# A fused attention and bilinear feed-forward kernel: idle matmuls on another constant, weights in twelve loads, merged reciprocals and a new written order

## The chip, the cores and the metric

The kernel runs on one core of a Trainium2 chip. The metric is the time of one execution on the device in microseconds, the median of the runs shown. A profile is one execution, recorded instruction by instruction; its span runs from the first to the last instruction. Engines are named as in the profile: PE is TensorE's matrix multiplication, PEld its loading of weights (the stationary operand), DVE is VectorE, ACT is ScalarE, POOL is GpSimd, and SP is SyncE, which only issues DMAs here.

## The reference

Eight batches of eight heads, 576 queries and keys, head width 64. The attention is causal and has a forgetting gate f, whose running sum of logarithms is added to the scores as a decay. Its output, 4608 tokens of 512 features, goes through a bilinear feed-forward layer of inner width 1536. All inputs and the output are float32.

```python
scores = q @ k.T / sqrt(D)
cum = cumsum(log(clip(f, 0.0001, 1.0)))
scores = where(causal, -1e9, scores + cum[:, None] - cum[None, :])
attn = exp(scores - scores.max(-1)); attn = attn / (attn.sum(-1) + 1e-9)
x = attn @ v                          # heads beside each other: 4608 x 512
out = ((x @ w_a) * (x @ w_b)) @ w_out
```

## The kernel before

Matrix work is in float16 with float32 sums. Heads are taken in pairs: four pairs per batch, 32 in all, numbered t = 0 to 31, the two heads of a pair on partitions 0-63 and 64-127. The 576 queries of a pair are five blocks: blocks 0 to 3 of 128 queries, and block 4 of the last 64 (both heads in one tile). Block i has 128(i+1) keys, block 4 all 576.

For a pair, TensorE makes the scores (tiles sc, lines 538 and 550). For batch 0 the decay is added by matmuls and VectorE only takes the row maximum (line 645). From batch 1 on, one VectorE instruction adds the decay row, held for every partition in the tile spread, writes the sum to S and keeps the maximum in the small tile st (line 673). ScalarE takes the exponential into PA (blocks 0 to 2) or PB (blocks 3 and 4) and the row sum into st (lines 700 and 704). VectorE then takes the reciprocal of the sums, block by block (lines 712 and 714), and each block of each head is multiplied by it, nearly always on GpSimd ("normalisation", line 725). The normalised probabilities are transposed: by TensorE (psP) for batch 0 and one part of batch 1, otherwise by a DMA issued by SP into PTA and PTB. The product with v (pv, pvx, lines 768 and 783, "PV") follows, and its copy goes into xT, which holds the attention's output with features on partitions. The k, q and v of later batches are loaded, cast and transposed (psT, line 358) in between; those of batch 0 are loaded by GpSimd's queue, with a cast on the way.

The feed-forward layer takes groups of 256, 384 or 512 tokens as they are ready: psa = x w_a and psb = x w_b, ScalarE copies psa to a (line 288), VectorE multiplies psb by it into ht (line 1072), and pso = ht w_out (helper on line 74, which splits each matmul into two halves of columns). The last 1024 tokens use fewer products of sums of blocks (lines 1218 to 1363: wg, wb, og, ob, om).

The weights w_a, w_b and w_out are loaded by GpSimd's queue with a cast to float16 (function weights, line 509). w_a and w_b come in two stretches of columns, 0 to 512 and 512 to 1536, each in two halves of rows: eight loads, and three more for w_out. Of the twelve inner blocks of 128 columns, a feed-forward step with block f waits for the loads whose columns cover that third.

At the start TensorE has nothing to multiply; 24 steps named wake, each of four matmuls of 512 columns into a tile that nobody reads, stand in its order before and between the first real steps. They read the identity, which two GpSimd steps build.

The order of the work is written out. The function first makes a list of some 2,480 steps (class Op), each with its engine or the engines to choose from. The string ORDER numbers them in the order in which they are issued, so that each engine's queue holds its own steps in that order and waits, in order, for what each needs. CHOICE picks the engine where there are several, and SLOTS picks the buffer for each tile. The durations written in Op calls and the priorities served to make these strings; they have no effect when the kernel runs.

```python
        for lo, hi in ((0, 512), (512, DF)):          # function weights
    with tc.manual_schedule():
        for o in order:
            o.fn(o.eng)
```

Of the kernel before, what the change touches and what calls it, by code (L numbers as in the profile page):

```python
# [10 lines left out]
FP16 = mybir.dt.float16  # L11
# [14 lines left out]
def kernel(  # L26
# [11 lines left out]
    nc = tc.nc  # L38

    B, H, S, D = q.shape  # L40
# [29 lines left out]
    warm = perm.tile([128, 1], FP32, tag="warm", name="warm")  # L70

# [33 lines left out]
    def paddings():  # L105
# [36 lines left out]
        PA:012302310231023102310231023102310231;PB:01101010101010101010101010101010;S:0101101001101001101010110  # L142
        0110101010101001010101010101010010011010100101001000100010011011010011010100110101001101010110101010101
        ;a16:0120120120120120120120120120120121021021201201201201021021020210210120120121021021021021021;bc:012
        0120120120120120120120120120;ff:01230123013200031230120131312313102312022101012133203012301230123012301
        2301302132021021230230201230231021301230123012012302131231231021230130230132103120301010312013210321023
        1023023102310321321302130213013210321032103102132132012312312303021021023103120313201302130230123120312
        0302102012120102301310210213023123201321301321320120320312032130213021302301213021303210312303021021320
        130213201302312031203120321032102301;ht:0123456789abcd0123456789abcd0123456789ab01cd2345678a019b23cd456
        8017a29bd345c0168279a34bd015c2;n16:01101001011000101001010101010101;n32:0120102102102102010202121220120  # L150
        110102121101202201201201202120;nv:0101010101;osb:010101010100101010101010101001;qd:01010101010101010101
        0101;sc:01010101010101010101010110100101011000101010110010010101101010101011010101010101010100101011101
        10010101011001010111010101010101010101010101010101;st:01234510324510324510324510324510
# [555 lines left out]
    def do_recip(t, i):  # L709
        st = T[("st", t)]  # L710
        if i == 4:
            nc.vector.reciprocal(out=st[:, 28:29], in_=st[:, 18:19])
        else:
            nc.vector.reciprocal(out=st[:, 20 + 2 * i:22 + 2 * i], in_=st[:, 10 + 2 * i:12 + 2 * i])  # L714
# [106 lines left out]
    def attention(t, base):  # L821
# [75 lines left out]
        direct_ex = {}  # L897
        for g, gi in [(g, groups[g]) for g in ((0, 1, 3, 2) if t in MASKP else (0, 1, 2, 3))]:
            qk, su = qk_of[g], None
            for i in gi:  # L900
# [55 lines left out]
                rc = Op("DVE", 0.16, lambda _, i=i: do_recip(t, i), es, prio=prio(g))  # L956
                st_users.extend(es + [rc])
                for h in range(1 if i == 4 else 2):
                    nm = Op(None, {"POOL": NORM[i]} | ({"ACT": 0.2 + 0.00082 * 128 * (i + 1)} if b in EARLY else {}), lambda e, i=i, h=h: do_norm(e, t, i, h), [rc], prio=prio(g),
                            name=f"norm{t}.{i}")  # L960
                    st_users.append(nm)
                    pu[part].append(nm)
                    norms.setdefault(part, []).append(nm)
                    norm_of.append((i, nm))
# [593 lines left out]
    for n in cuts:  # L1558
# [5 lines left out]
        0 1 29 30 46 2 52 62 5 3 31 37 32 38 33-36 39 40 42 41 53 47 58 4 43 267 262 279 6-9 54 48 10 56 50 44  # L1564
# [25 lines left out]
        1792-1794 618 493 491 1795 492 494 631 702 707 653 654 703 697 1797 569 704 626 623 632 619 1796 1798  # L1590
# [3 lines left out]
        1822 677 1823 1825 670 1826 669 646 1824 657 716 676 718 717 658 1827 1829-1831 709 719 723 767 671 681  # L1594
# [131 lines left out]
```

## Time and profile before

| | |
|---|---|
| timed runs | 392.8, 396.06 and 396.86 us; median 396.06 |
| profiled execution | span 394.4 us (its time outside the span is not given) |
| TensorE clock granted, mean | 0.999 of full speed |
| busy share PE, PEld, DVE, ACT, POOL | 97%, 64%, 83%, 76%, 71% |
| DMA | 76.88 MB, 195 GB/s over the span |

In the profile's lists, a group "L714 DVE RECIPROCAL st<-st 128x2" is an instruction of line 714 that reads and writes the tile st; x128 is the count, then come the sum of busy time in us, the mean of one in ns, and the idle time of the engine just before them with the engine, tile and line that ended it. Matmuls overlap each other, so a busy TensorE is not one at its peak. The chain of waits goes back from the last instruction, at each step to what released it. In the list of DMA issues the last number is the median time from issue to landing.

### The profile page before, as it was taken

Reading aid. Unit: us, or ns where it says so; the run is one execution under the profiler, and the core shown is the slowest. Engines: PE = TensorE matmul, PEld = TensorE weight load, DVE = VectorE, ACT = ScalarE, POOL = GpSimd, SP = SyncE. Lnnn points to the kernel's source line nnn. Section 1 sums busy time; section 2 is a strip of 40 time slices with the busy share of each in tenths; the row PEclk is TensorE's granted clock in tenths of the full one; section 3 lists DMA queues with packets and bytes.
Section 4 is the critical chain, followed back from the end, with each engine's and each line's share of the span. In section 5 each row is a group of like instructions: output and inputs, shape, how many; then the busy total and the mean of one; then the engine's idle time right before and its main releaser. Section 6 shows DMA issues by size and latency. Waiting matters only on the chain.

```text
span 394.4 us, 14909 instructions
## 1 busy us (share of the span) xinstructions
PE 381.1 (97%) x5816; PEld 253.9 (64%) x5816; DVE 329.1 (83%) x1035; ACT 299.4 (76%) x826; POOL 281.0 (71%) x482
## 2 busy tenths in 40 slices
PE   7899999999998999999899999999999999999996
PEld 3557887968765665655555655555555667666796
DVE  7888898998996888788788888757898899987992
ACT  4998999999886878868888588779899672556331
POOL 8689686768867689874899769578976891267600
PEclk9999999999999999999999999999999999999999
DMA  7999999999999999999998999999998898100005
GB/s 121 251 202 170 144 154 223 228 278 275 208 222 215 220 282 247 281 187 277 260 237 255 262 207 229 206 244 263 226 226 195 169 182 178 55 1 2 2 2 214
DMA packets 147190, 76.88 MB, mean 195 GB/s; under 512 B 124336, under 2 KB 128176, under 8 KB 147120
## 3 DMA queue, kind: packets, MB, share of 16 engines
q1 hardware_dynamic: 132824, 68.79, 77.9%
q0 software_dynamic: 14256, 7.08, 14.7%
q8 instruction: 45, 0.74, 0.8%
q14 instruction: 25, 0.20, 0.2%
q10 hardware_dynamic: 40, 0.07, 0.1%
HBM read 52.05 MB, written 9.58 MB: 156 GB/s over the span
## 4 chain that ended last, share of the span: by engine, by line
PE 73%; DMA 11%; DVE 5%; POOL 4%; ACT 3%; issue 2%; ACTq 0%; DVEq 0%; POOLq 0%
PE psa L74 15%; PE psb L74 15%; PE pso L74 13%; PE wg L74 5%; DMA PTA<-PA 5%; PE wb L74 4%; PE sc L550 3%; PE og L74 3%; DMA PTB<-PB 3%; PE pvx L768 3%; PE psT L358 2%; DVE S L673 2%; DMA wb<-in_moe_w_b_dram 2%; POOL PA L725 2%; PE wake L74 2%
## 5 line engine op out<-in xcount | busy, mean ns | idle before, releaser
L673 DVE CUSTOM_DVE_ANT_0 S<-sc,spread 64x576 f32<-64x576 f32 (+4 forms) x232 | 125.5, 561 | 14.5 <-ACT PA L704 4.8
L725 POOL TENSOR_SCALAR PA<-PA,st 128x256 f16<-128x256 f16 (+2 forms) x180 | 85.0, 481 | 9.6 <-DVE st L714 6.0
L74 PE MATMUL psb<-xT,wb 128*64 128x512 f16 (+2 forms) x864 | 88.7, 332 | 0.4 <-DVE ht L1072 0.2
L704 ACT ACTIVATE PA<-S,st 128x256 f16<-128x256 f32 (+2 forms) x168 | 84.1, 503 | 6.4 <-DVE st L673 5.8
L74 PE MATMUL psa<-xT,wa 128*64 128x512 f16 (+2 forms) x864 | 88.9, 333 | 0.0
L74 PE MATMUL pso<-wout,ht 128*64 128x512 f16 x672 | 81.8, 381 | 0.0
L725 POOL TENSOR_SCALAR PB<-PB,st 128x512 f16<-128x512 f16 (+1 forms) x90 | 63.6, 713 | 25.3 <-DVE st L714 8.8
L74 PEld LDWEIGHTS <-wb 128*64 128x64 f16 x960 | 55.9, 110 | 24.9 <-issue 1.8
L74 PEld LDWEIGHTS <-wa 128*64 128x64 f16 x960 | 55.2, 110 | 24.7 <-issue 2.2
L1072 DVE TENSOR_TENSOR ht<-psb,a 128x512 f16<-128x512 f32 (+1 forms) x90 | 57.5, 648 | 7.2 <-PE psb L74 5.1
L288 ACT CAST a<-psa 128x512 f16<-128x512 f32 (+1 forms) x90 | 49.4, 550 | 18.0 <-PE psa L74 15.8
L74 PEld LDWEIGHTS <-ht 128*64 128x64 f16 x696 | 38.3, 110 | 26.8 <-issue 2.2
L704 ACT ACTIVATE PB<-S,st 128x512 f16<-128x512 f32 x56 | 40.2, 720 | 3.2 <-DVE st L673 2.7
L704 ACT ACTIVATION_READ_ACCUMULATOR PA<-S,st 128x1 f32 x168 | 32.1, 191 | 0.0
L630 POOL TENSOR_SCALAR_AFFINE_SELECT spread<-spread 128x768 f32<-128x768 f32 x24 | 20.8, 866 | 14.0 <-DMA spread<-cum_d 13.9
L700 ACT ACTIVATE PB<-S,st 128x576 f16<-128x576 f32 x28 | 21.7, 776 | 10.7 <-DMA PTB<-PB 4.1
L768 PEld LDWEIGHTS <-nv 128*64 128x64 f16 x640 | 21.8, 110 | 8.5 <-DMA PTA<-PA 2.3
L673 DVE CUSTOM_DVE_ANT_1 S<-sc,spread 128x256 f32<-128x256 f32 x48 | 19.7, 419 | 7.5 <-ACT PB L704 1.6
L1273 POOL TENSOR_TENSOR hy<-wu 128x512 f16<-128x512 f32 x9 | 11.6, 1302 | 19.7 <-DVE wu L1273 19.6
L714 DVE RECIPROCAL st<-st 128x2 f32<-128x2 f32 x128 | 18.1, 156 | 7.2 <-ACT PA L704 3.6
L673 DVE DVE_READ_ACCUMULATOR2_ANT st<- 128x1 f32 (+1 forms) x280 | 22.8, 81 | 0.0
L550 PE MATMUL sc<-kT,qT 64*128 64x512 f16 (+4 forms) x144 | 21.0, 326 | 1.2 <-ACT kT L288 0.4
(156 smaller groups left out, 692.8 us busy)
## 6 DMA issues: line engine op xcount, KB each, us to landing
spread<-cum_d SPq DMA_DIRECT2D x24, 576.0 KB, 6.4
q<-in_q_dram SPq DMA_DIRECT2D x14, 576.0 KB, 5.3
k<-in_k_dram SPq DMA_DIRECT2D x14, 576.0 KB, 5.4
out_dram<-osb SPq DMA_DIRECT2D x29, 256.0 KB, 4.0
v<-in_v_dram SPq DMA_DIRECT2D x24, 256.0 KB, 5.8
wout<-in_moe_w_out_dram POOLq DMA_DIRECT2D x3, 512.0 KB, 8.0
nv<-in_v_dram POOLq DMA_DIRECT2D x8, 128.0 KB, 5.1
wa<-in_moe_w_a_dram POOLq DMA_DIRECT2D x2, 512.0 KB, 7.5
```

What stands on the lines that cost most here:

```text
L74: nc.tensor.matmul(out=out[r], lhsT=lhsT[:, r], rhs=rhs, **kw)
L288: nc.scalar.copy(out=out_, in_=in_)
L550: nc.tensor.matmul(out=dst, lhsT=lhsT, rhs=rhs, start=start, stop=stop, skip_group_check=True)
L630: nc.gpsimd.affine_select(out=c[:, :, 0:SM].rearrange("p h (j k) -> p h j k", k=128), in_=c[:, :, SM:2 * SM].rearrange("p h (j k) -> p h j ...
L673: nc.vector.tensor_tensor_reduce(out=o, in0=x, in1=y, scale=-1.0, scalar=3e38, op0=ADD, op1=MIN, accum_out=m)
L700: nc.scalar.activation(out=p_blocks(t, 4), in_=T[("s" if direct else "z", t, 4)], func=EXP, bias=st[:, 8:9], scale=sign, accum_out=st[:, 1 ...
L704: nc.scalar.activation(out=p_blocks(t, i)[:, :, h, :], in_=(T[("s", t, i)][:, h, :] if direct else T[("z", t, i)][:, h * n:h * n + n]).rea ...
L714: nc.vector.reciprocal(out=st[:, 20 + 2 * i:22 + 2 * i], in_=st[:, 10 + 2 * i:12 + 2 * i])
L725: VEC[e].tensor_scalar(out=p, in0=p, scalar1=st[:, c:c + 1], scalar2=1.0, op0=MUL, op1=MUL)
L768: nc.tensor.matmul(out=o[HP[h], 128 * i:128 * i + 128], lhsT=vt[:, j, pr + NP * h, :], rhs=pt[:, base_blk[i] + 2 * block_at(t, i, j) + h, ...
L1072: nc.vector.tensor_tensor(out=ht[:, 0:n_], in0=T.pop(("psb", t0, fbs))[:, 0:n_], in1=T.pop(("a16", t0, fbs))[:, 0:n_], op=MUL)
L1273: VEC[e].tensor_tensor(out=out_, in0=x, in1=y, op=op)
```

## The change

Four things change, and with them the three strings.

The idle matmuls read a new tile, spark, of two columns that VectorE sets to 1.0, broadcast to the shape of both operands; they no longer wait for the identity. Their number stays.

w_a and w_b are loaded in three stretches of 512 columns, so in twelve loads; w_out's three stay.

The reciprocals of a pair are merged: for batches 0 and 1 blocks 0 and 1 share one, block 2 has its own, and blocks 3 and 4 share one; for the other batches blocks 0 to 2 share one and blocks 3 and 4 share one. The reciprocal is issued for all its columns of st at once, after the exponentials of all its blocks, and all its normalisations wait for it.

SLOTS, ORDER and CHOICE are new throughout. In ORDER the steps of the last 1024 tokens stay in nearly the same sequence on TensorE. GpSimd's queue now begins with the identity and then the loads of batch 0's k and q; weight loads stand at other places among its normalisations. On VectorE and ScalarE some evictions change sides: VectorE makes 28 instead of 22 copies of transposed q and k, and ScalarE 16 instead of 11 copies of PV results.

```diff
+    spark = perm.tile([128, 2], FP16, tag="spark", name="spark")
...
-            mm_halves(x, ident16, ident16[:, 0:1].to_broadcast([128, 512]), start=True, stop=True, skip_group_check=True)
+            mm_halves(x, spark[:, 0:1].to_broadcast([128, 128]), spark[:, 0:1].to_broadcast([128, 512]), start=True, stop=True, skip_group_check=True)
...
+    o_s = Op("DVE", 0.1, lambda _: nc.vector.memset(spark, 1.0), prio=-302, name="spark")
...
-        o = Op("PE", 0.427, lambda _: wake(2), [o_i], prio=-290, mode="full", name=f"wake{n}")
+        o = Op("PE", 0.427, lambda _: wake(2), [o_s], prio=-290, mode="full", name=f"wake{n}")
...
-        for lo, hi in ((0, 512), (512, DF)):
+        for lo, hi in ((0, 512), (512, 1024), (1024, DF)):
...
-    def do_recip(t, i):
+    RGROUPS = {True: [(0, 1, 2), (3, 4)], False: [(0, 1), (2,), (3, 4)]}
+
+    def do_recip(t, blocks):
         st = T[("st", t)]
-        if i == 4:
-            nc.vector.reciprocal(out=st[:, 28:29], in_=st[:, 18:19])
-        else:
-            nc.vector.reciprocal(out=st[:, 20 + 2 * i:22 + 2 * i], in_=st[:, 10 + 2 * i:12 + 2 * i])
+        c0, c1 = 2 * blocks[0], 9 if blocks[-1] == 4 else 2 * blocks[-1] + 2
+        nc.vector.reciprocal(out=st[:, 20 + c0:20 + c1], in_=st[:, 10 + c0:10 + c1])
...
-                rc = Op("DVE", 0.16, lambda _, i=i: do_recip(t, i), es, prio=prio(g))
...
+                for blocks in RGROUPS[b not in EARLY]:
+                    if i not in blocks or not all(x in ex_of for x in blocks):
+                        continue
+                    rc = Op("DVE", 0.16, lambda _, blocks=blocks: do_recip(t, blocks), sum((ex_of[x] for x in blocks), []),
+                            prio=prio(g), name=f"rc{t}.{blocks[0]}")
+                    st_users.append(rc)
+                    for x in blocks:
+                        for h in range(1 if x == 4 else 2):
+                            nm = Op(None, {"POOL": NORM[x]} | ({"ACT": 0.2 + 0.00082 * 128 * (x + 1)} if b in EARLY else {}),
+                                    lambda e, x=x, h=h: do_norm(e, t, x, h), [rc], prio=prio(g), name=f"norm{t}.{x}")
...
     ORDER = """
-        0 1 29 30 46 2 52 62 5 3 31 37 32 38 33-36 39 40 42 41 53 47 58 4 43 267 262 279 6-9 54 48 10 56 50 44
...
+        0 3 22 15 14 20 26 30 2 4 12 1 32 47 49 31 53 48 63 33 34 38 39 35 36 45 51 54 59 37 5 40 44 41 43 55 57
...
```

More of the change, by code (lines that the diff above doesn't have):

```diff
@@ L147 @@
[L147 to L151, printed above, removed]
@@ L152 @@
-        0101;sc:01010101010101010101010110100101011000101010110010010101101010101011010101010101010100101011101
-        10010101011001010111010101010101010101010101010101;st:01234510324510324510324510324510
+        PA:012302310231021302130213012301230123;PB:01010101010101010101010101010101;S:010101010101011001101001
+        010100100101010110010010110100100101101001010010010101000100110100101001010101001010010011010101010101
+        01;a16:0120102102001020101201201102010120101002100120012010120120012010112010010100200120101010010;bc:
@@ new lines @@
+        0120120120120121201201201021012;ff:0123000123011123112000000123333320012223011200012230120123012321002
+        130231203123212101121230213201231203210230123013201300122312130213012301213021301203120132103120123123
+        012032032012031023102312301230213020130101230121020123021301201230123012031023102012013203013012013012
+        301231201312301212132012301201301213012031230121312312301012123012010120312031203102103201301010202031
+        1203012032103123021012031020312013201320123;ht:0123456789abcd0123456789ab0123cd4560172389ab01234567c89
@@ L154 @@
+        d01a234567b8c012345679abd0123456789ac0;n16:01010101010111010100110001101010;n32:0121202112012012202112
+        121201010120120120121010201120120121012;nv:0101010101;osb:010101011010101010101010101001;qd:0101010101
+        01010010010101;sc:010101010101010101101001100101010101101001001001011000100110100001010101011011001101
+        0101011001101010110100010101101110101001000101010010101001010;st:01234501234501234501234501234501
     """
@@ L955, in attention @@
                 su.extend(es)
-                rc = Op("DVE", 0.16, lambda _, i=i: do_recip(t, i), es, prio=prio(g))
[L957 to L964, printed above, removed]
+                st_users.extend(es)
+                ex_of[i] = es
+                for blocks in RGROUPS[b not in EARLY]:
[8 more added lines that the diff above has]
+                                    lambda e, x=x, h=h: do_norm(e, t, x, h), [rc], prio=prio(g), name=f"norm{t}.{x}")
+                            st_users.append(nm)
+                            pu[part_of(t, x)].append(nm)
+                            norms.setdefault(part_of(t, x), []).append(nm)
+                            norm_of.append((x, nm))
         trs, ptu = {}, {}
@@ new lines @@
+        89 107 159 160 124 125 233 108 185 109 190 27 110 19 111 260-262 167 168 263 23 82 112 186 202 203 113
[3 rows of a table added]
+        1633 272-274 305 306 275 308 198 1631 218 236 239 237 240 1634 1636 1638 1635 149 161 162 80 1640 1637
+        1639 70 69 84 169 128 201 199 238 241 243 170 86 339 307 342 343 346 347 200 1641 269 281 270 344 345
+        349 283 340 129 355 1642-1644 126 356 1645 348 242 387 358 388 171 300 302 303 390 490 350 353 389 392
+        397 393 309 1646 1647 357 405 394 407 172 311 395 399 1648 1649 396 398 406 206 282 207-209 352 408 291
@@ new lines @@
+        312 409 249 127 214 250 215 1650 1653 316 317 301 255 256 1654 212 313 1651 1652 310 496 314 318 434 435
+        484 436 410 315 319 320 322 321 327 213 1655 1656 341 366 491 492 367 494 354 362 363 493 1658 1659 359
+        304 323-325 244 251 326 364 365 1660 1662 1661 368 252 369 1663 391 412 413 351 1664 1666 416 1667 437
+        360 438 510 1668 370 1670 371 372 257 485 1657 417 414 551 418 1665 400 402 1669 415 439 442 443 361 495
+        447 258 446 516 440 455 456 511 444 449 330 331 1672 1671 1673 457 497 1674-1677 373 458 377 332 333 374
@@ new lines @@
+        448 328 557 329 459 441 466 445 450 419 420 462 463 421 422 486 375 376 487 488 1678 1680 1679 464 1681
+        465 508 467 513 517 521 1682 404 468 506 411 518-520 523 1683 501 380 381 515 509 401 403 423 425
+        525-527 382 383 1684 469 453 1685 1687 424 452 691 507 522 524 426 472 536 537 451 498 500 499 528 1688
+        378 379 470 454 473 474 460 428 429 1689 478 479 554 552 558 563 471 1690 427 502 560 565 559 561 592
+        692 514 562 564 503-505 1692 1693 512 598 461 529-531 539 1694 540 538 541 1696 1695 566 567 679 680 542
[4 rows of a table added]
@@ new lines @@
+        1719 621 676-678 1726-1728 622 616 1730 1732 1734 686 1729 575 623 1731 1733 636 640 641 644 645 615 624
+        613 685 701 572 1736 1738 1735 693 687 648 649 1739 694 695 741 1737 625 642 651 549 550 1740 1742 1741
+        576 650 638 573 589 659 643 660 647 646 652 1743 1744 1746 1747 1745 1748 1750 1751 886 703 707 661 1720
+        712 627 653 709 708 711 713 714 654 637 655 1752-1755 710 635 662 664 663 706 665 1756 1758 715 717 716
[5 rows of a table added]
+        794 791 796 877 790 792 787 873 808 809 1789 1790 793 795 1791-1793 1795 1797 723 1784 1794 1796 1785
@@ new lines @@
+        1798 881 882 738 797-801 826 1778 972 766 776 810 721 830-833 784 786 811 835 805 722 812 804 1799 1801
+        1800 834 874 807 1803 763 1802 1804 836 837 1786 1787 724 814 806 875 828 849 850 1805 1807 1806 698
+        1808 1809 1811 896 825 779 813 815 816 838 839 699 1810 840 878 880 827 841 842 848 1813 803 1815 1812
+        890 879 852 853 1814 851 1816-1820 854 855 737 739 891 893 897 846 899 901 902 1059 762 905 906 898 1821
[10 rows of a table added]
+        1091 1088 929 955 1041 1095 930 1096 1089 1093 1090 968 1065 1885-1887 1889 1250 1888 1890 1891 1017
@@ new lines @@
+        1092 1033 1073 1097 1076 1094 1098 1892 1036 1006 1075 1037 1074 1893 1035 1015 1042 1044 1043 1045 1085
+        1106 1107 1895 1897 1899 1894 1896 1122 1007 1008 1066 1010 1898 1077 1851 1082 1108 1900-1902 1244 1903
+        993 1038 995 1124 1128 1132 1129 1130 1134 1905 1906 1067 1068 1162 1131 1069 1084 1904 1907 994 1910
+        1911 1046 1048 1034 1047 1133 1135 1163 1009 1109 1110 970 1111 1908 1050 1909 1078 1049 1136-1139 1099
[5 rows of a table added]
+        1941 1214 1938 1940 1216 1184 1942 1943 1164 1191 1193 1192 1194 1945-1947 1195 1218 1254 1155 1157 1156
@@ new lines @@
+        1159 1271 1276 1262 1219 1949 1213 1220 1951 1199 1944 1948 1198 1221 1215 1217 1119 1120 1950 1311 1208
+        1229 1230 1196 1952-1955 1273 1277 1231 1278 1281 1279 1145 1280 1205 1222 1197 1200 1207 1283 1957-1959
+        1224 1956 1232 1234 1256 1282 1233 1924 1235 1223 1960 1236 1961 1962 1284-1286 1141 1239 1963 1965 1238
+        1228 1966 1275 1967 1969 1237 1296-1298 1968 1226 1971 1970 1964 1272 1312 1288 1972 1919 1201 1317 1202
[4 rows of a table added]
+        1985 1988 1982 1290 1242 1243 1451 1344-1346 1369 1370 1334 1399 1986 1396 1400 1404 1401 1295 1269 1460
@@ new lines @@
+        1408 1409 1402 1410 1411 1989-1991 1308 1434 1993 1995 1357 1378 1379 1444 1997 1994 1996 1291 1998-2001
+        2003 2005 1405 2002 2004 1347 1349 1435 1406 2007 2006 2008 1398 1403 1992 1407 2009 2011 2013 1412 1331
+        1380 2010 1419 1336 1420 2014 1421 2012 1293 1415 1436-1438 1266 1356 1395 1371 1374 1397 1422 1307 1423
+        1354 1381 1383 1425 2330 2015-2017 2019 2018 1424 1382 1426 2021 1501 2020 1377 2023 2025 2022 2024 1332
+        1452 1384 1373 1267 1417 1309 1446 2026 1335 1416 1348 1310 1461 1463 1467 1471 1469 1987 1468 1470 2331
@@ new lines @@
+        1473 1385 1458 2027 2028 1472 1474 2029-2031 2033 1475 1477 1476 1478 1428 1418 2032 1375 2034 1466 1502
+        1542 1504 1508 1509 1512 1513 1413 1414 1430 1510 1511 1387 1465 1515 1372 1486 1487 2041 2035 2037 2036
+        2039 1350 1514 2038 1516 1517 1386 1351 1388 1390 2042 1447 2040 1519 1518 1520 1429 1453-1455 1462 1505
+        1376 1389 1445 1464 1489 1490 2043 2046 2044 2124 1427 1431 1479 1488 1492 1507 1548 1491 1506 2047 1583
+        2048 2051 2049 2045 1527 1528 1503 1530 1493 1494 1485 1448 1450 1449 2050 1531 1529 1532 1533 1391 1392
@@ new lines @@
+        2052 1543 1545 1549 1551 1553 1495 1496 1498 1554 1524 1534 1537 2053 2056 2054 1557-1560 1432 1550 1584
+        1586 1590 1594 1591 1595 2057-2059 1433 2061 2063 2065 2067 1555 1552 1556 1561 1592 1535 1536 1539 1597
[3 rows of a table added]
+        2087-2089 1563 2091 2093 2090 2092 2094 1585 1612 1613 2095 2096 2126 1611 1605 2097 2099 2098 2100 1615
+        2127 2060 1457 1497 1459 1499 1500 1578 2101 2103 2105 1606 2107 1614 1616 1538 1540 2102 1608 2109 1577
+        2110 2104 1541 2106 2108 1576 2055 2111 2130 2114-2117 2129 2125 2128 2134 2132 1579-1581 2119 2120 1603
@@ L1680 @@
+        PAPPPPPDDDAAPPPPPAPPDAAADAAADDAADADAAAAADDAADADADAADADDDDADDDDAADAAAAAAAAAADDDADAAAAADADAAADDAADAADAAD
+        DAAAAAADAAADAAAADAAAAAAAAADDAAAADDAAAAAAAAAAAAAAAAAAAAAADAAAAAAAAAAAAAA
     """
```

33 lines of the change are left out of this document (6 added, 27 removed), and 140 rows, old and new, of the table ORDER.

## The prediction

> **What bounds the kernel now.** I read the page first, then the busy time by stretches of ten microseconds, then TensorE's waits, then the chain of waits in the first 48 us, and last the groups and DMA issues that price the edits.
>
> ```profile
> span 394.4 us, 14909 instructions
> PE 381.1 (97%) x5816; PEld 253.9 (64%) x5816; DVE 329.1 (83%) x1035; ACT 299.4 (76%) x826; POOL 281.0 (71%) x482
> DMA  7999999999999999999998999999998898100005
> PE 73%; DMA 11%; DVE 5%; POOL 4%; ACT 3%; issue 2%; ACTq 0%; DVEq 0%; POOLq 0%
> ```
>
> TensorE is busy 97% of the span and carries 73% of the chain; the DMA row is full until slice 33. The change keeps every matmul (864 psa, 864 psb and so on come from loops that the diff doesn't touch, and 24 wakes stay 24). So it can gain only what TensorE now idles, or stretches in which TensorE is filled with wakes.
>
> ```profile
> 0.00:10.00 10.00, 7.20 (x108) 3.66 (x110) 7.62 (x26) 4.33 (x7) 8.52 (x25) 1.00 0.79 122
> 10.00:20.00 10.00, 8.84 (x192) 5.28 (x186) 8.65 (x16) 9.70 (x38) 6.59 (x12) 1.00 1.14 253
> 20.00:30.00 10.00, 9.37 (x162) 5.82 (x160) 8.58 (x23) 9.23 (x30) 8.91 (x18) 1.00 1.00 199
> 30.00:40.00 10.00, 9.78 (x198) 7.38 (x196) 8.62 (x17) 8.99 (x22) 9.18 (x15) 1.00 1.08 172
> ...
> 390.00:394.40 4.40, 0.76 (x14) 0.49 (x10) 0.57 (x2) 0.37 (x1) 0.00 (x0) 0.95 0.65 242
> sum 394.40, PE 381.11 PEld 253.92 DVE 329.11 ACT 299.38 POOL 281.01; mean PE 9.53 PEld 6.35 DVE 8.23 ACT 7.48 POOL 7.03
> ```
>
> The columns are the stretch, its length, then busy time of PE, weight loads, DVE, ACT and POOL. TensorE is busy 35.19 of the first 40 us (idle 4.81) and 0.76 of the last 4.4 (idle 3.64). The 350 us between hold 381.11 - 35.19 - 0.76 = 345.16, so 4.84 are idle there. All idle time is 13.3 us; the 3.64 at the end are last copy and store, which both written orders do in the same order.
>
> ```profile
> PE wake L74 <- POOL ident masks.py:199: 2.8, 1, 2.8
> PE pvx L768 <- DMA PTA<-PA: 2.0, 4, 0.7
> PE sc L538 <- DVE ht L1072: 1.1, 1, 1.1
> PE sc L74 <- DVE xT L292: 1.0, 1, 1.0
> ...
> PE psb L74 <- DVE ht L1072: 0.2, 1, 0.2
> PE psb L74 <- DMA wb<-in_moe_w_b_dram: 0.2, 1, 0.2
> ```
>
> These are TensorE's waits. The 2.0 (transposed probabilities), the 1.1 + 1.0 + 0.2 on VectorE and the 0.2 on a weight load make 4.5 of the 4.84 idle in the middle. That is the whole prize there.
>
> ```profile
> 20.70 0.14 DVE st L714 x2
> ...
> 21.58 0.62 POOL wa L509
> ...
> 23.10 0.60 POOL wa L509
> 23.70 0.61 POOL wb L509
> ...
> 26.63 0.60 POOL wb L509
> ...
> 27.74 0.59 POOL wa L509
> ...
> 31.41 0.61 POOL wa L509
> 32.06 0.60 POOL PA L725
> ...
> 32.70 0.53 PE psP L74 x12
> ...
> 35.87 0.79 PE psa L74 x13
> 36.66 0.51 POOL PA L725
> 37.17 7.87 DMA wb<-in_moe_w_b_dram
> ```
>
> This is the chain that leads to the first feed-forward matmul. From 20.7 to 32.7 us it runs along GpSimd: six issues of weight loads (3.63 us) stand between the normalisations that the transposes wait for.
>
> **Idle matmuls.** They wait for one VectorE memset instead of two GpSimd steps, so they start near 1.1 us, not 2.8. Nothing real can start sooner for it, since the first transposes wait for q and k:
>
> ```profile
> 7.21 0.69 PE L358 MATMUL psT<-ident,q 64*64 64x64 f16 x18
> ...
> 10.25 0.47 PE L358 MATMUL psT<-ident,q 64*64 64x64 f16 x18
> ```
>
> The early 18 take 0.69 us, the same form three microseconds later 0.47. If the clock is up when they come, two such groups gain 0.4 us; if not, nothing. GpSimd now builds the identity ahead of all loads and not behind the first, which delays k by about the identity's time and leaves q where it was; q landed last. In the new order one score step stands two transposes sooner. Bounds -1.0 to +0.3; I take -0.4. The Trainium skill, "TensorE: Matmul & The Clock Gate", section "The HAM clock gate", says that the full clock comes after about 3.4 us of sustained work whatever the count, on a window that runs freely. By that the 0.4 would come in most executions and not in all; the rows here show the slow and the fast duration but not the window.
>
> **Weights in twelve loads, and the new order on GpSimd.** Rows for prices:
>
> ```profile
> L725 POOL TENSOR_SCALAR PA<-PA,st 128x256 f16<-128x256 f16 (+2 forms) x180 | 85.0, 481 | 9.6 <-DVE st L714 6.0 <-issue 2.5
> L509 POOL DMA_DIRECT2D wa<-in_moe_w_a_dram x4 | 2.6, 656 | 0.0
> L304 POOL DMA_DIRECT2D nv<-in_v_dram x10 | 8.7, 872 | 0.0
> ...
> wa<-in_moe_w_a_dram POOLq DMA_DIRECT2D x2, 512.0 KB, 7.5
> ...
> wa<-in_moe_w_a_dram POOLq DMA_DIRECT2D x2, 256.0 KB, 5.4
> ...
> 14.03 0.37 POOL L725 TENSOR_SCALAR PA<-PA,st 128x128 f16<-128x128 f16 x1 [2.84 <-DVE st L714]
> ...
> 21.00 0.58 POOL L725 TENSOR_SCALAR PA<-PA,st 128x384 f16<-128x384 f16 x1 [1.49 <-DVE st L714]
> ```
>
> Four loads more are 4 x 0.66 = 2.6 us of GpSimd. I counted both written orders up to the last normalisation that holds the first psa: before it is pair 2's third block, after the change pair 3's. Before: 17 normalisations, 6 weight issues, 2 loads of v. After: 19, 8 and 3, and one low part of the decay row that was VectorE's, which I price as a normalisation. That is 3 x 0.48 + 2 x 0.66 + 0.87 = 3.6 us more, and GpSimd idled 2.84 + 1.49 = 4.3 us there, which the new order fills: three weight issues and a cast of q come ahead of its first normalisation. So the gate falls at about 32 to 33.5 us instead of 32.7. Behind it TensorE had 3.2 us to the first psa (32.70 to 35.87); now a transpose, one PV step and one score step remain, about 2 us, since the transposes of pair 0's wide part have moved ahead. First psa at 34 to 36: I take -0.8, bounds -2 and +1.5. If the cover of those 4.3 us is not there (rows of the reciprocal come later than now), all 3.6 show.
>
> By the same count the last load of the middle third of wb is issued some 1 us later than the one that landed 7.87 us after 37.17, but a third lands 2 us quicker (5.4 against 7.5). The 0.2 us wait goes or grows to 1: zero taken. Against twelve loads speaks the Trainium skill, "DMA: Bandwidth & Descriptors", section "Bandwidth", which wants loads batched to 1 MiB and gives each some 2 us of fixed time. By it four more loads would cost up to 8 us if they were waited for one by one; the rows show loads of two sizes only 2.1 us apart, in flight beside each other.
>
> **Merged reciprocals.**
>
> ```profile
> L714 DVE RECIPROCAL st<-st 128x2 f32<-128x2 f32 x128 | 18.1, 156 | 7.2 <-ACT PA L704 3.6 <-ACT PB L704 3.2
> L712 DVE RECIPROCAL st<-st 128x1 f32<-128x1 f32 x32 | 4.8, 154 | 3.4 <-ACT PB L700 3.2
> ```
>
> 160 become 8 x 3 + 24 x 2 = 72, and width hardly prices (154 for one column, 156 for two), so VectorE loses 88 x 0.156 = 13.7 us and part of 10.6 us of waits. Eight evictions (six of q and k, two of the decay row) come to it and six other copies and one subtraction leave, which nearly cancels. It isn't the bound; on TensorE's path are its 1.1 + 1.0 + 0.2. I take half: -1.2, bounds -2.3 and 0. The new wait: for pairs 8 to 31 the reciprocal of blocks 0 to 2 waits for the last exponential of block 2. Behind it on VectorE queue the next score reductions and the feed-forward products; for it wait up to six normalisations on GpSimd, then the transpose, then PV. Four normalisations that ran beside the exponentials now run behind them: up to 4 x 0.48 = 1.9 us later for each pair. What hides it: between a pair's block-2 scores and its PV I count on average 25.4 feed-forward steps of psa, psb and pso in the new order against 23.9, larger in 13 of 24 pairs and smaller in 9. At 0.86 us for a step of eight,
>
> ```profile
> 146.02 0.86 PE psa L74 x8
> ```
>
> that is 1.3 us more lead against up to 1.9 more chain. So the 2.0 us of waits on PTA stay: 0 taken, bounds -2 and +6 (each of the four doubling, and four new ones of 1).
>
> **Sum.** -0.4 - 0.8 - 1.2 = -2.4 us against the span of 394.4: 392.0. The timed runs are 392.8, 396.06 and 396.86; the page gives the profiled execution's span and not its time, so I put the median's 1.7 us above the span as what lies around it: **393.7 us**.
>
> **The rivals.** *A, all waits go.* VectorE's relief and the longer leads close most of the 4.8 us in the middle, and the start gains its bound of 2 to 3: 394.4 - 4 - 3 + 1.7 = 389. For it: the waits are few, each with a named cause the order moves. Against: a fixed order makes its own. Chance 0.28. *B, the transposes come late.* It starts at the merged reciprocal: where a pair's lead is shorter than its chain, PV waits. Pairs 19, 30 and 31 have leads of 17, 17 and 19 steps in the new order, the least being 18 before. It decides once about six pairs more wait 1 us each, on a DMA row that is full: 393.7 + 6 + 1 = 401. For it: PTA and PTB hold most of the chain's 11% of DMA. Chance 0.22. *C, the gain is eaten.* The weights rule above as a mechanism: the added issues (2.6 us) lie ahead of the normalisations or of the load that psb waits for: 393.7 + 2.6 = 396.3. Chance 0.12. The forecast itself, 391 to 397, has 0.38.
>
> **The numbers.** One per cent of 396.06 (about what a measurement here can tell from no change) puts the edges at 392.1 and 400.0. Faster: A's 0.28 and a quarter of the forecast, 0.37. Slower: B without its mildest cases, 0.2. Same: 0.43. The range runs from A's 389 less 2 us for its start bound to B's 401: 387 to 401.
>
> **What would show it.** Idle matmuls from about 1.1 us and early transposes near 0.47; the first psa at 34 to 36; TensorE's waits on VectorE under 1.2 in sum; PTA waits near 2; reciprocals x72 near 0.16. Wrong if PTA waits reach 6, or the first psa passes 37.5, or if TensorE's idle time between 40 and 390 falls under 1.

## The result and the profile after

Over 20 executions of each on one chip the changed kernel took 398.11 us in the median (394.6 to 404.31) and the kernel before 394.04 (392.31 to 397.39): a ratio of 1.0087, 95% interval 1.0057 to 1.0116. The ratios in this document leave out executions more than 1.5% above the quickest of the same kernel, so they can differ from the quotient of the medians. I had forecast 393.7. The time lies in the range of 387 to 401 and within 1% of no change, but it moved the other way: some 3.4 us were lost where I expected 2.4 to be gained.

The profiled execution of the changed kernel took 395.56 us. Its page opens so (span, busy time of the engines, the row of the DMA engines):

```profile
span 393.9 us, 14803 instructions
PE 381.0 (97%) x5816; PEld 254.5 (65%) x5816; DVE 326.4 (83%) x951; ACT 296.7 (75%) x819; POOL 287.2 (73%) x490
DMA  7999999999999999999999999999998696100005
```

TensorE has the same 381 us to do, VectorE 84 instructions fewer. The busy time by stretches, in the columns of the prediction (stretch, length, PE, weight loads, DVE, ACT, POOL, clock, DMA):

```profile
0.00:10.00 10.00, 6.83 (x132) 3.82 (x134) 7.22 (x27) 5.46 (x9) 8.63 (x22) 1.00 0.78 123
10.00:20.00 10.00, 9.03 (x166) 4.78 (x162) 8.08 (x15) 8.54 (x34) 9.19 (x18) 1.00 1.32 280
20.00:30.00 10.00, 9.31 (x145) 5.30 (x147) 9.58 (x20) 8.98 (x29) 9.56 (x21) 1.00 1.26 236
30.00:40.00 10.00, 9.82 (x205) 7.43 (x201) 8.34 (x16) 7.56 (x17) 9.08 (x14) 1.00 0.94 165
40.00:390.00 350.00, 345.75 (x5184) 233.12 (x5180) 293.12 (x876) 265.77 (x733) 250.75 (x418) 1.00 0.93 194
390.00:393.90 3.90, 0.24 (x5) 0.00 (x0) 0.05 (x1) 0.37 (x1) 0.00 (x0) 0.87 0.60 222
```

TensorE is idle 5.01 us in the first 40 (4.81 before), 4.25 in the 350 that follow (4.84 before) and 3.66 at the end (3.64). Next TensorE's longest waits (engine, tile and line, what it waited for, us in total, times, longest):

```profile
PE sc L540 <- ACT osb L290: 1.3, 2, 0.7
PE sc L552 <- ACT qT L288: 1.3, 1, 1.3
PE psb L75 <- DVE osb L294: 1.2, 1, 1.2
PE wake L75 <- DVE warm L216: 1.0, 1, 1.0
PE pso L75 <- ACT a L290: 0.7, 1, 0.7
PE wb L75 <- DVE wu L1282: 0.6, 1, 0.6
PE sc L552 <- DVE qT L292: 0.6, 1, 0.6
```

The waits on PTA that stood high in the list of before are gone. In their place stand copies of TensorE's results (osb, qT and a on ScalarE, osb and qT on VectorE) and a product, wu. The wait for the identity (2.8) is now one of 1.0 for the memset (the row names warm, which VectorE sets right behind spark). By this one execution the two kernels look alike; yet the medians differ by 4 us. The two profiled executions lie on opposite sides of their medians: that of before at about 396.1 us (its span and the 1.7 us that the other traces have outside theirs), 2 above, and that of the changed kernel 2.6 below.

### The profile page after: what moved, and what is told of

Read it like the earlier page. It is cut to its first block, busy times and chain, and to the rows that moved or that the text cites. A ratio compares the mean times of both kernels' runs of the same rounds, so it can differ in the third digit from the quotient of the medians.

```text
span 393.9 us, 14803 instructions
## 1 busy us (share of the span) xinstructions
PE 381.0 (97%) x5816; PEld 254.5 (65%) x5816; DVE 326.4 (83%) x951; ACT 296.7 (75%) x819; POOL 287.2 (73%) x490
## 4 chain that ended last, share of the span: by engine, by line
PE 52%; POOL 7%; DMA 4%; issue 2%; ACT 2%; DVE 2%; POOLq 0%; ACTq 0%; DVEq 0%
PE pso L75 12%; PE psa L75 11%; PE psb L75 10%; PE wg L75 4%; DMA PTB<-PB 3%; PE wb L75 3%; PE og L75 3%; PE pvx L770 2%; POOL PA L727 2%; POOL PB L727 2%; DMA out_dram<-osb 1%; PE om L75 1%; PE sc L540 1%; PE sc L75 1%; PE psT L360 1%
## 5 line engine op out<-in xcount | busy, mean ns | idle before, releaser
L727 POOL TENSOR_SCALAR PA<-PA,st 128x128 f16<-128x128 f16 (+2 forms) x181 | 86.6, 490 | 15.7 <-DVE st L716 9.8
L75 PE MATMUL pso<-wout,ht 128*64 128x512 f16 x672 | 80.9, 380 | 0.9 <-ACT a L290 0.7
L727 POOL TENSOR_SCALAR PB<-PB,st 128x512 f16<-128x512 f16 (+1 forms) x92 | 64.5, 707 | 19.6 <-DVE st L716 7.4
L75 PEld LDWEIGHTS <-wb 128*64 128x64 f16 x960 | 55.0, 110 | 28.4 <-issue 4.7
L75 PEld LDWEIGHTS <-ht 128*64 128x64 f16 x696 | 39.7, 110 | 28.1 <-issue 3.6
L294 POOL CAST k<-k 128x1152 f16<-128x1152 f32 x14 | 16.0, 1140 | 5.8 <-PE psb L75 3.5
```

Of the source, the lines that this page charges most:

```text
L75: nc.tensor.matmul(out=out[r], lhsT=lhsT[:, r], rhs=rhs, **kw)
L294: VEC[e].tensor_copy(out=out_, in_=in_)
L727: VEC[e].tensor_scalar(out=p, in0=p, scalar1=st[:, c:c + 1], scalar2=1.0, op0=MUL, op1=MUL)
```

## The experiments

Ratios are to the kernel before, run on the same chip in the same rounds. TensorE's granted clock is the mean of an execution.

**The changed kernel again, and with the early hole filled.** In the 20 executions of the changed kernel the mean granted clock went from 0.983 to 1.0 and the time with it: at 0.999 or above six executions took 394.6 to 396.77 us (median 395.8), at 0.995 and 0.996 six took 395.89 to 400.21 (397.6), at 0.991 or below eight took 398.5 to 404.31 (400.2). The start of the profiled execution shows where a clock could fall (start, us, engine, line, operation; the idle time before it in brackets):

```profile
1.00 4.41 PE L75 MATMUL wake<-spark 128*64 128x512 f16 x24 [1.00 <-DVE warm L216]
5.55 0.47 PE L360 MATMUL psT<-ident,k 64*64 64x64 f16 x18
6.36 0.47 PE L360 MATMUL psT<-ident,q 64*64 64x64 f16 x18 [0.33 <-DMA q<-in_q_dram]
7.16 0.47 PE L360 MATMUL psT<-ident,k 64*64 64x64 f16 x18 [0.33 <-DMA k<-in_k_dram]
8.92 0.34 PE L552 MATMUL sc<-kT,qT 64*128 64x256 f16 x4 [1.29 <-ACT qT L288]
```

Of the 96 idle matmuls (24 steps of four) the first 24 stand here ahead of the transposes, and the next eight come only at 10.37. The old order had 20 ahead of the transposes and eight more between them and the first score. The 24 start 1.8 us sooner than before, and so they also end sooner. From 5.41 to 8.92 TensorE runs three groups of 0.47, 1.41 us out of 3.51; in this execution the clock held all the same. I ran the changed kernel as it is, and with ten idle matmuls more in this hole (they compute nothing that is used).

```diff
     order = laid_out()
+    named = {o.name: o for o in order}
+
+    def led(name, n):
+        o = named[name]
+        fn = o.fn
+        o.fn = lambda e: (wake(n), fn(e))
+
+    for name, n in (("pt0q0", 1), ("pu0k0", 1), ("qk0.0", 3)):
+        led(name, n)
```

> The changed kernel once more, beside the others on one chip. In its profile TensorE streams for only about a quarter of the 3.4 us from 5.2 to 8.6 us, and its executions have mean granted clocks from 0.983 to 1.0, the time longer where the clock is lower. Gap theory (the early idle stretch lets the clock fall in some executions): about 1.009 of the time of before, mean clocks again spread down to 0.98. Order theory (waits of the new order and of the merged reciprocals later on): 1.009 too, but the time does not follow the clock. Constant theory (the all-ones operand of the idle matmuls doesn't count as activity): 1.009 too.

> The changed kernel with ten idle matmuls more in the early stretch: two before the transposes of q, two before those of the second k, six before the first score step. Nothing else differs. Gap theory: mean clock 0.998 or more in nearly all executions, and 0.996 to 1.003 of the time of before, some 2 to 4 us quicker than the changed kernel. Order theory: unchanged at 1.009 (or slower by the added matmuls, under 1 us). Constant theory: unchanged at 1.009, clocks still down to 0.98, since the added matmuls read the same constant.

As it is: 397.6 us, ratio 1.0113 (1.0057 to 1.0168), clock below 0.997 in 5 of 6 executions. Filled: 396.23 us, 1.0075 (1.0041 to 1.0108), clock below 0.997 in 1 of 12, like the kernel before (2 of 23). The filling gives the clock back. The 1.4 us between the medians fit that, though the two intervals overlap and the six unfilled times don't follow the clock (395.2 to 399.62 where it fell, 396.59 where it did not). The "about a quarter" of the first expectation is 1.61 of 3.40 us by the profile's busy time. The profile of the changed kernel run again caught the fall itself:

```profile
1.00 5.04 PE L75 MATMUL wake<-spark 128*64 128x512 f16 x24 [1.00 <-DVE warm L216]
...
8.92 0.50 PE L552 MATMUL sc<-kT,qT 64*128 64x256 f16 x4 [1.21 <-ACT qT L288]
...
14.31 0.34 PE L552 MATMUL sc<-kT,qT 64*128 64x256 f16 x4 [0.56 <-DVE qT L292]
```

The same four score matmuls take 0.50 us at 8.92 and 0.34 at 14.31. By stretches (the column before the last two is the granted clock):

```profile
5.00:8.60 3.60, 2.20 (x62) 1.19 (x58) 3.43 (x8) 2.77 (x5) 3.13 (x8) 0.99 1.07 162
8.60:12.00 3.40, 3.08 (x64) 2.11 (x65) 1.73 (x4) 2.17 (x7) 3.12 (x11) 0.51 1.08 236
```

Here the idle matmuls end at 6.04, and up to 8.92 TensorE is busy 1.23 of 2.88 us. From 8.5 on, before the hole ends, the clock is half for 3.4 us. One such stretch lowers the mean of a 390 us execution by 0.0044, which is the step between the clocks seen (1.0, 0.996, 0.991, 0.987). Means of 0.991 and less then stand for two such stretches and more. No execution of the changed kernel with two was profiled, so where the others stand is not shown.

**The converse: a hole in the kernel before.** Its idle matmuls between the first transposes and about 11 us were left out.

```diff
     order = laid_out()
+    for o in order:
+        if o.name in ("wake5", "wake6", "wake7", "wake8"):
+            o.fn = lambda _: wake(0)
```

> The kernel before, with the sixteen idle matmuls of wake5 to wake8 left out (their tiles are still taken), which stand between TensorE's first transposes and about 11 us; the idle matmuls compute nothing that is used. Nothing else is changed. Theory of the granted clock (an early stretch in which TensorE is mostly idle costs one or more stretches of a lower clock): mean granted clocks below 0.995 in most executions and a ratio of 1.003 to 1.010. Rival, that the lower clocks of the changed kernel come from something else in its order: clocks of 0.998 to 1.0 as before and a ratio of 0.998 to 1.002.

395.93 us, 1.0067 (1.004 to 1.0093), clock below 0.997 in 8 of 11 executions against 1 of 16 of the kernel before. The clock fell and the cost came, with nothing of the new order in the kernel; the clock fell less far than expected (two of 11 executions under 0.995). Not all of the cost need be clock: the two executions recorded at 1.0 took 395.63 and 397.16, no less than the others. In its profile the slow stretch stands behind the hole again:

```profile
8.33 0.34 PE L550 MATMUL sc<-kT,qT 64*128 64x256 f16 x4
...
10.62 0.47 PE L358 MATMUL psT<-ident,k 64*64 64x64 f16 x18 [0.71 <-DMA k<-in_k_dram]
...
12.66 0.50 PE L550 MATMUL sc<-kT,qT 64*128 64x256 f16 x4 [1.02 <-DVE kT L292]
```

**The idle matmuls' constant by itself.** Once in the kernel before (only the operand and its memset are new), once undone in the changed kernel (identity as operand again, and issued first on GpSimd).

```diff
# the kernel before
-            mm_halves(x, ident16, ident16[:, 0:1].to_broadcast([128, 512]), start=True, ...
+            mm_halves(x, spark[:, 0:1].to_broadcast([128, 128]), spark[:, 0:1].to_broadcast([128, 512]), start=True, ...
# the changed kernel
+    order.remove(o_i)
+    order.insert(0, o_i)
```

> The kernel before with the first part of the change alone: its idle matmuls read the VectorE constant and start some 1.7 us sooner; order, loads and reciprocals as before. Gap theory: the first twenty idle matmuls end near 5.5 us while the first transposes still wait for q until about 7.2, so an idle stretch of 1.5 to 2 us opens; some executions get a clock under 0.998, time 1.000 to 1.008 of before. Order theory: 1.000. Constant theory: 1.008, clocks down to 0.98.

> The changed kernel with its idle matmuls reading the identity as before, which is now built first and ready at about 1.4 us; all else as changed. Gap theory: 1.005 to 1.010 of before with clocks down to 0.98, since the stretch is as empty. Order theory: 1.009. Constant theory: 1.000, clocks at 0.998 or more.

Alone in the old order: 393.83 us, 0.9989 (0.9952 to 1.0027). Undone in the new one: 398.26 us, 1.0114 (1.0057 to 1.0171), clocks 0.985 to 0.996. So the constant neither gains nor loses by itself that these runs can tell, although the earlier start opens a wait of 1.5 us for q and the clock was below 0.997 in 3 of 12 executions. Taking it away does not close the hole, since the identity too is ready at 1.44 there; the place of the idle matmuls in the order makes it. The profile of the first kernel is a second picture of the old order, taken in the quickest of its twelve executions (391.29 us). Its longest waits and its middle:

```profile
PE psT L360 <- DMA q<-in_q_dram: 1.5, 1, 1.5
PE sc L540 <- DVE ht L1074: 1.3, 1, 1.3
PE wake L75 <- DVE warm L217: 1.0, 1, 1.0
```

```profile
40.00:386.00 346.00, 343.90 (x5152) 230.71 (x5148) 295.15 (x954) 266.13 (x733) 248.72 (x415) 1.00 0.93 198
```

Only 2.1 us are idle in the middle, and one wait of 1.3 makes most of it. The 2.0 us on PTA and the 1.0 on xT that I counted as standing waits are 0.2 and nothing here. The kernel with twelve loads below, profiled in an execution near its median (393.44 us), agrees: 2.2 idle, 0.2 on PTA and 0.2 on xT. But idle time in the middle goes with the execution as well as with the order. From 40 us to 3.9 before the end it is 2.1, 2.2, 4.8 and 5.2 us in four traces of the old order (the last is the kernel with the hole, 396.38 us) and 2.7, 3.0, 4.25 and 5.0 in four of the new (395.2, 395.46, 395.56 and, filled, 396.74 us).

**Twelve loads alone, and eight in the new order.** In the kernel before the four 1024-column loads were each issued as two of 512; in the filled kernel the last two thirds of each weight became one load again.

```diff
# the kernel before
+            for lo in range(0, n, 512) if n == 1024 else (None,):
+                c = slice(None) if lo is None else slice(lo, lo + 512)
+                nc.gpsimd.dma_start(out=dst[:, :, c], in_=src[:, :, c])
# the filled kernel
+                    lo_, hi_ = (512, DF) if lo == 512 else (lo, hi)
```

> The kernel before with twelve weight loads alone: each load of columns 512 to 1536 is issued as two of 512, one behind the other at the same place. Loads theory (2.6 us more of GpSimd on the chain to the first feed-forward step): 1.003 to 1.006 of before. Order theory: 0.998 to 1.003.

> The changed kernel with the ten idle matmuls more, and eight weight loads again: columns 512 to 1536 in one load at the place of the middle third's. Loads theory: 0.3 to 0.6% under the 1.0075 of the twelve-load version, so 1.002 to 1.004 of before. Order theory: 1.005 to 1.010.

Alone: 394.33 us, 1.0015 (0.9986 to 1.0044). Back to eight: 397.22 us, 1.0103 (1.0067 to 1.0139), no better than the filled kernel's 1.0075. The number of loads is not the cause.

**Merged reciprocals in the old order.** For pairs 8 to 31 the last reciprocal of each group writes the whole group, and the normalisations that stood ahead of it come right behind it; once with both groups, once with blocks 3 and 4 alone.

```diff
     order = laid_out()
+    for t in range(8, 32):
+        for blocks in ((0, 1, 2), (3, 4)):      # second kernel: ((3, 4),)
+            rcs = [o for o in order if o.name in {f"rc{t}.{i}" for i in blocks}]
+            last = rcs[-1]
+            early = [o for o in order[:order.index(last)] if o.name in {f"norm{t}.{i}" for i in blocks}]
+            last.fn = lambda _, t=t, blocks=blocks: merged(t, blocks)
+            order = [o for o in order if o not in rcs[:-1] and o not in early]
+            at = order.index(last) + 1
+            order[at:at] = early
```

> The kernel before with merged reciprocals alone, for pairs 8 to 31 (blocks 0 to 2, and 3 and 4): 72 reciprocals fewer, the merged one at the place of its group's last, normalisations that stood ahead of it moved right behind it; order otherwise as before. Merge theory (normalisations and transposes come late): 1.004 to 1.008 of before, with several us of waits on transposed probabilities. Relief theory of the prediction: 0.994 to 0.998. Order theory (the merging is neutral, the loss lies in the new order's own waits): 0.998 to 1.003.

> The kernel before with the reciprocals of score blocks 3 and 4 alone merged for the query tiles from 8 on, and the normalisations of block 3 moved behind the merged reciprocal. Merging both groups cost 5.2%. If the price goes with the number of blocks that wait (one of three waiting blocks here), the ratio is 1.010 to 1.025. If the group of blocks 0, 1 and 2 makes the price alone (its first normalisations wait for two more rounds of exponentials), the ratio is 0.998 to 1.006. If the last group does (the transposes of PTB come straight behind it), it is 1.03 or more.

Both groups: 413.7 us, **1.0517** (1.0467 to 1.0566). Blocks 3 and 4 alone: 405.64 us, 1.0323 (1.0272 to 1.0374), above all the sizes but that of the last rival: the group at the end of a pair makes the larger part. With both, GpSimd stands still for the merged reciprocals, and TensorE for a transpose and for GpSimd:

```profile
POOL PA L725 <- DVE st L1697: 13.5, 7, 3.5
POOL PB L725 <- DVE st L1697: 10.3, 6, 3.5
```

```profile
PE pvx L768 <- DMA PTB<-PB: 5.5, 2, 4.4
PE sc L74 <- POOL qd L610: 2.2, 1, 2.2
```

The second kernel shows how such a wait is paid twice. TensorE waits for 4.1 us (337.0 to 341.1) and 1.1 more, and the clock is half from 339.1 to 349.4:

```profile
PE pvx L768 <- DMA PTB<-PB: 5.2, 2, 4.1
```

```profile
337.00:347.00 10.00, 4.81 (x68) 3.63 (x67) 5.37 (x10) 1.28 (x2) 2.84 (x3) 0.61 0.52 111
```

**Single reciprocals in the new order.** Three ways, all in the filled kernel: single ones at the merged one's place; each block's own two VectorE steps after its last exponential; the same with the block's normalisations right behind it.

```diff
# at the same place
-        c0, c1 = 2 * blocks[0], 9 if blocks[-1] == 4 else 2 * blocks[-1] + 2
-        nc.vector.reciprocal(out=st[:, 20 + c0:20 + c1], in_=st[:, 10 + c0:10 + c1])
+        for i in blocks:
+            c0, c1 = 2 * i, 9 if i == 4 else 2 * i + 2
+            nc.vector.reciprocal(out=st[:, 20 + c0:20 + c1], in_=st[:, 10 + c0:10 + c1])
# early: behind the block's last exponential, past two VectorE steps
+                own = Op("DVE", 0.16, lambda _, t=t, i=i: single(t, (i,)), name=f"r{t}.{i}")
+                order.insert(at, own)
# early, with the normalisations
+                mine = [o for o in order if o.name == f"norm{t}.{i}"]
+                order = [o for o in order if o not in mine]
+                at = order.index(own) + 1
+                order[at:at] = mine
```

> The changed kernel with the ten idle matmuls more, and each merged reciprocal issued as single ones at the same place (88 instructions of about 0.16 us more on VectorE, 13.7 us in sum; waits unchanged). If VectorE's time were worth anything: 1.009 to 1.013 of before. If it lies off the path: 1.006 to 1.009, as without the split.

> The changed kernel with the ten extra idle matmuls of the earlier run in the early gap, and each block's reciprocal issued by itself, two VectorE steps after the block's last exponential, in place of the merged one. The normalisations and everything else keep their places. Theory that the merged reciprocals hold up what follows (normalisations, casts, masks, transposes): most of the 0.75% that is left at full clock goes, a ratio of 1.000 to 1.004, although VectorE has some 13 us more to do. Rival, that the new order itself costs it, whatever the reciprocals do: 1.0075 to 1.012, as with the merged reciprocals replaced by single ones at the same place (1.0123).

> As the kernel with early single reciprocals, and with each block's normalisations moved right behind its own reciprocal as well. Theory of the merged reciprocals: 0.998 to 1.004, no slower than with the normalisations in their old places, since what waits is released earlier still. Rival of the order: 1.0075 or more; if it is slower than the kernel that only splits the reciprocals, the places of the normalisations matter more than the time at which they could start.

At the same place: 398.01 us, 1.0123 (1.0079 to 1.0167). That is 0.2% above the merged version with eight loads, run beside it (1.0103), and 0.5% above the one with twelve (1.0075), which these runs can't tell apart. So VectorE's 88 instructions are worth little; what waiting for the merged ones costs in the new order is not tested by this, since the single ones wait as long. Early: 407.92 us, 1.0394 (1.0351 to 1.0436). Early with the normalisations: 447.61 us, 1.1389 (1.1344 to 1.1434). Both theories had expected far less, and the two runs don't decide between them: I had put the reciprocals at places that VectorE reaches before the exponentials are done, so it stands there, and all evictions and products queue behind it.

```profile
DVE st L1708 <- ACT PA L706: 15.8, 25, 1.2
DVE st L1708 <- ACT PB L706: 7.1, 12, 1.1
```

They show how little room there is on either side: reciprocals placed too early by a few VectorE steps cost some 3% over the filled kernel (1.0394 against 1.0075), and with the normalisations moved as well 13%.

## Why the prediction was wrong

Three gains were summed and none of them shows in the time, and two costs of the new order had no term: a hole among the idle matmuls, and copies held up on ScalarE.

**The prize was mis-sized.** The 4.84 us idle in the middle belong to an execution 2 us above the median of twenty. In the two quicker traces of the old order 2.1 and 2.2 us are idle there. Of VectorE's 1.1 + 1.0 + 0.2, on which the relief of -1.2 was counted, the 1.1 and the 0.2 stand there too (1.3 and 1.2; 0.2), the 1.0 does not; of the 2.0 on PTA 0.2 is left. With 2.1 or 2.2 idle, rival A's closing of 4 us was out of reach.

**Idle matmuls, taken at -0.4, bounds -1.0 to +0.3.** The parts that I named came: a start at 1.00 us, transposes of 0.47 from the first, the first score at 8.92 (9.70 before). Alone the edit is within noise, 0.9989. The step that failed is "Nothing real can start sooner for it", from which I went straight to the sum. I had counted that 24 steps stay 24 and not looked at where they stand: in the new order the first 24 matmuls end sooner and nothing replaces them before 8.92. By the medians that costs about 1.4 us (397.6 against 396.23 filled), by the clocks of the first 20 executions about 2.3 (398.11 against 395.8 at full clock), outside my bounds either way. The clock's behaviour agrees with the Trainium skill, "TensorE: Matmul & The Clock Gate", section "The HAM clock gate", in the length of the slow stretch (3.4 us) and in its being a matter of chance from one execution to the next. The Trainium skill warns on the same page, section "HAM oscillation", of idle gaps over some 3.4 us; the trace here is stricter: in the execution with the clock of 0.51 the longest single idle time up to the fall and across it was 1.21 us.

**Weights and GpSimd's order, taken at -0.8.** The first feed-forward matmul came at 37.1, not at 34 to 36 (35.87 before; below the 37.5 that I called wrong):

```profile
L75 PE MATMUL psa<-xT,wa x864: 269/326/403, 37.1 to 324.0; 128*64 128x512 f16 x77, 128*64 128x256 f16 x58, 128*64 128x384 f16 x38
```

The 4.3 us of GpSimd's idle time were filled as I had counted, and the gate held: the last normalisation of a 128x384 block ends at 33.3 us, inside 32 to 33.5. But behind it stood more than one transpose, one PV step and one score step, and 3.8 us instead of 2:

```profile
34.17 0.53 PE L75 MATMUL psP<-ident,PA 128*64 128x128 f16 x12
34.50 0.92 PE L75 MATMUL psP<-ident,PB 128*64 128x128 f16 x26
35.23 0.53 PE L75 MATMUL psP<-ident,PA 128*64 128x128 f16 x12
```

So the -0.8 did not come. That the 1.2 us by which the first psa is later were lost is not shown, since TensorE did other work meanwhile: it is idle 5.01 us of the first 40, 0.2 more than before. The thirds did not land quicker:

```profile
wb<-in_moe_w_b_dram POOLq DMA_DIRECT2D x6, 256.0 KB, 7.4
wa<-in_moe_w_a_dram POOLq DMA_DIRECT2D x6, 256.0 KB, 6.5
```

That is 7.4 and 6.5 us for a third, where the old kernel's rows had 5.4 for a third and 7.5 for two. No psb waited for them, so the zero for that wait was right, and so was leaving rival C's 2.6 us out (1.0015 for the loads alone).

**Merged reciprocals, taken at -1.2 on VectorE and 0 on PTA.**

```profile
L716 DVE RECIPROCAL st<-st 128x6 f32<-128x6 f32 (+3 forms) x72 | 12.1, 173 | 6.6 <-ACT PB L706 4.8 <-ACT PA L706 1.5 <-ACT PB L702 0.3
```

The 72 are busy for 12.1 us, at 173 ns each where I put 156, against 18.1 + 4.8 for the 160 before. VectorE has only 329.1 - 326.4 = 2.7 us less to do in all; copies that moved to it take part of the difference (of the main forms 15 instead of 9 into qT, 7 instead of 5 each into osb and spread, but 8 instead of 13 of pvx into xT), and the rest is not accounted for. TensorE's waits on VectorE (warm aside) are 2.4 now, not under 1.2. On PTA I had expected the 2.0 to stay; no wait on it is left in this trace, but 0.2 in the two quicker traces of the old order shows that there was little to lose. The step that failed is that I followed the late probabilities only to TensorE. They also come out on ScalarE: the exponentials of blocks 3 and 4 write one of two PB buffers, and must wait until the transposes have read it.

```profile
ACT PB L702 <- DMA PTB<-PB: 5.0, 6, 1.4
```

In the profile of before and in that of the constant alone this row reads

```profile
ACT PB L700 <- DMA PTB<-PB: 4.1, 3, 2.9
ACT PB L702 <- DMA PTB<-PB: 1.3, 1, 1.3
```

The sum alone does not separate the orders: it is 1.2 to 4.1 in four traces of the old order and 2.0 to 6.1 in six of the new. The spacing does. From the records of pairs 8 to 31 (mean of 24): the first normalisation of PB starts 2.4 us behind its last exponential in the changed kernel, 0.9 with the constant alone; the last one ends 7.1 behind it against 6.3; and it ends 8.2 us ahead of the buffer's next use against 8.6, at most 6.1 in six pairs against two, with the transposes (5 to 6 us in the chain of waits) still to come between. Three more traces of each order agree (the start at 2.4 against 0.9 to 1.0, the end at 7.1 to 7.2 against 6.3 to 6.4). While ScalarE stands, the copies queued behind it stand too. Three of these stands on ScalarE, in the timeline (the bracket is the idle time before the row):

```profile
107.61 0.78 ACT L702 ACTIVATE PB<-S,st 128x576 f16<-128x576 f32 x1 [0.91 <-DMA PTB<-PB]
137.09 0.78 ACT L702 ACTIVATE PB<-S,st 128x576 f16<-128x576 f32 x1 [1.44 <-DMA PTB<-PB]
208.75 0.77 ACT L702 ACTIVATE PB<-S,st 128x576 f16<-128x576 f32 x1 [1.37 <-DMA PTB<-PB]
```

And TensorE's rows with the longest waits in the same 200 us:

```profile
109.22 0.84 PE L75 MATMUL psb<-xT,wb 128*64 128x384 f16 x8 [1.17 <-DVE osb L294]
140.43 0.51 PE L540 MATMUL sc<-kT,qT 64*128 64x128 f16 x10 [0.64 <-ACT osb L290]
210.14 1.92 PE L75 MATMUL pso<-wout,ht 128*64 128x512 f16 x16 [0.74 <-ACT a L290]
```

The first of TensorE's three has another cause: the copy of osb that it waits for stood on VectorE for 1.49 us until a store had freed its buffer. The second and third come 3.3 and 1.4 us behind a stand, and the chain of waits leads from it to them. The third comes again in all six traces of the new order and in none of the four of the old. It is 0.63 to 0.64 us shorter than the stand ahead of it each time (in five of the six the profile puts the stand's end down to PTB, in one to GpSimd, where the chain of waits has PTB). The shortest is 0.46 behind 1.09; the longest is this, in the kernel with single reciprocals at the merged one's place:

```profile
211.15 0.77 ACT L702 ACTIVATE PB<-S,st 128x576 f16<-128x576 f32 x1 [2.67 <-DMA PTB<-PB]
212.53 2.60 PE L75 MATMUL pso<-wout,ht 128*64 128x512 f16 x16 [2.04 <-ACT a L290]
```

There the clock also falls to half, from 213.6 to 217.0 us. So the step from ScalarE's stand to TensorE's wait is shown, at 0.5 to 2.0 us an execution at this one place. That the stand comes from the merging, and that this chain and not another of the new order's moves makes the rest of the loss at full clock, was not tried; a third PB buffer would tell.

**The rivals.** B's mechanism is real and large: 5.2% in the old order. In the new order no PV step waits for more than 0.2 us in any of its traces with merged reciprocals; that the longer leads do it, which I held against B, is not shown. I had asked only where TensorE meets the transposes, not where ScalarE does. A and C did not come. The case that came was not on the list: a hole ahead of the first score, and evictions held up by an engine that has time to spare. The lower edge of my range also took 2 us for the start from A's 389, which had them already.

**What adds up.** At full clock the filled kernel loses 0.75% (0.41 to 1.08), about 3 us. The six executions of the changed kernel at a clock of 0.999 or above lose less, 1.8 us (395.8 against 394.04). So the clock makes about 1.4 to 2.3 us of the loss and something else 1.8 to 3. That part is not read off the idle time of single profiles, which overlap between the orders; half a microsecond to two of it is the wait behind ScalarE's stand near 209 us. How it divides between the merged reciprocals and the rest of the new order stays open: merging costs 5.2% in the old order, what its delay costs in the new was not separated, and the kernel before is faster than every version that has either. None of the twelve kernels is faster than the kernel before by more than the runs can tell; the nearest is the constant alone.

## What to carry to other kernels

Price the waits of a stage by more than one execution: where the profiled time is above the median, part of its idle time is not the kernel's. When filler work is moved, ask what runs in the place that it leaves, as well as what it starts sooner. When a step is made to wait for more, follow its output to every engine that reuses the buffer: the wait may come out on one with idle time to spare, and reach the busy engine through the copies queued there.

## What was not expected of the hardware

TensorE's clock fell to half for 3.4 us in the last part of a stretch of 2.9 us in which TensorE was busy 43% and never idle for more than 1.21 us at once (the changed kernel run again, 6.04 to 8.92 us; the fall at 8.5). It is a matter of chance: in another execution of the same kernel it held through a stretch of 3.51 us at 40%. By the mean clocks it fell in 5 of 6 executions of one batch, and in 1 of 12 with ten idle matmuls more in that stretch. Later in a kernel a wait of 4.1 us came with 10.2 us at half clock, from its middle on. A 256 KB load landed in 5.4 us in one order and in 6.5 to 7.4 in another.
